# One new table of fixed instruction orders for the five queues of a top-k attention and two-MLP kernel

## The chip, the cores and the metric

The kernel runs on one core of a Trainium2 chip. The metric is the device time of one execution in microseconds (us), and lower is better. A core has a matrix engine (TensorE, PE in the rows), a vector engine (VectorE, DVE), a scalar engine (ScalarE, ACT), a general engine (GpSimd, POOL) and a queue that here only starts transfers (SyncE, SP). Each of the five runs its own list of instructions strictly in the order in which it stands; they wait for each other through semaphores.

## The reference

Two batches of 8 heads, 576 positions, 64 wide. Every attention row keeps its 32 largest scores; the result then goes through two MLPs, whose weights come as f32.

```python
def _attn_ref(q, k, v):                    # (2, 8, 576, 64)
    scores = scale * np.matmul(q, k.transpose(0, 1, 3, 2))
    kth = np.partition(scores, -32, axis=-1)[..., -32:-31]
    scores = np.where(scores >= kth, scores, -1000000000.0)
    scores = scores - np.max(scores, axis=-1, keepdims=True)
    attn = np.exp(scores)
    attn = attn / (np.sum(attn, axis=-1, keepdims=True) + 1e-09)
    return np.matmul(attn, v)
...
x = attn_out.transpose(0, 2, 1, 3).reshape(1152, 512)
h = x @ w_in;  x = np.maximum(0.01 * h, h) @ w_out        # 512 -> 2048 -> 512
h = x @ w_in2; out = (h * np.tanh(softplus(h))) @ w_out2  # 512 -> 2048 -> 512
```

## The kernel before

The 1152 tokens are cut into nine tiles of 128. For each tile the kernel makes the scores of eight heads, so there are 72 (tile, head) steps. Matrix products run on f16 halves: an f32 operand is split into a high and a low f16 part, and three f16 products stand for one f32 product. So each product of the MLPs comes as three lines: L822 to L824 (tile `ph`, 128 columns wide, the first layer of an MLP) and L831 to L833 (tile `y`, 512 columns wide, the second layer).

One step goes through all engines. `front` makes the scores on PE (L676, tile `sps`, two halves of 288 columns), and ACT copies them to `sc` (L678). `topk` runs on DVE: four times MAX8 (L691, eight maxima of each row) with three times MATCH_REPLACE8 between them (L694). ACT then takes the exponentials (L714, L715), and for the tiles from the fourth on casts them to f16 (L746, tiles `warena` or `eh`); POOL makes the low half (L747, L748); SP starts a transposing transfer (L754, tile `pts`); and PE multiplies with v (L760 to L764, tile `av`). When eight heads are done, DVE scales the tile to `x` (L778), which is then transposed to `xt` for the MLPs.

Beside the steps, up to about 230 us, the weights are prepared in groups: SP starts a transfer (`load_w`, L379), and ACT (L382), DVE (L389, L392, L395) and POOL (L331, adds) cut the words into parts; what they make lies in `warena`. A transfer needs a free staging place, which the adds of POOL on an earlier group free. The keys, `prep_k`, are normed and split, and for the later head pairs transposed by transfers on SP (L542 and L544, tile `kst`). The queries are read by L594 (`qr`), and keys and values by L501 and L505 (`rawkr`, `rawkv`).

What decides the order on each engine is neither the code order nor a scheduler: at the end of the kernel, `put_in_order(tc, ORDER)` takes for each of the five engines a string of numbers and ties every instruction to the one that the string names before it. A number is the place of an instruction in the order in which the code built it on that engine, and `a+n` stands for n in a row from a on:

```python
for run in runs.split():
    a, n = (run.split("+") + ["1"])[:2]
    for i in made[int(a):int(a) + int(n)]:
        if last is not None:
            tc.add_manual_dep(i, last.name, kind, reason="order")
        last = i
```

Of the kernel before, what the change touches and what calls it, by code (L numbers as in the profile page):

```python
# [19 lines left out]
        """20+2 19 22 25 28 23 29 27 26 24 35 42 36 43 31 30 32 39 41 46 33 44 47 45 40 37 48 38 49+7 57+2 60 56 34 62  # L20
# [4 lines left out]
        189 183 190+2 188 192+2 195+2 194 197+4""",  # L25
    "Activation":
        """1 6 2 7 4 3 5 9 8 20 17 16 45 11 18 10 12 21 46 13 19 14 27 22 15 28 23 47 24 29 39 25 50 40 49 33 48 41+2
# [30 lines left out]
        889 886+3 890+6""",  # L58
    "Pool":
        """0 2+3 6+2 11 28 30 8 10 5 16 34 31 29 15 9 12 33 19 14 32 35 18 20 13 23 17 21 36+2 24 26 39 38 25 60 27 22  # L60
# [1059 lines left out]
```

## Time and profile before

| what | us |
|---|---|
| median of three runs | 668.48 (668.25 to 670.13) |
| the profiled execution | 669.29 |
| its span, first to last instruction | 667.4 |
| around the span | 1.89 |
| mean granted clock of TensorE | 0.982 |

The profile is that of one execution; all times at which something starts are counted from the beginning of its span. The profiled execution is 0.81 us above the median. Matmuls overlap, so a busy PE is not PE at its peak: how full it is shows in the distance from start to start. In a timeline row, the bracket at the end gives how long the engine was idle before the instruction, and what ended that.

### The profile page before, as it was taken

Reading aid. Unit: us, or ns where it says so; the run is one execution under the profiler, and the core shown is the slowest. Engines: PE = TensorE matmul, PEld = TensorE weight load, DVE = VectorE, ACT = ScalarE, POOL = GpSimd, SP = SyncE. Lnnn points to the kernel's source line nnn. Section 1 sums busy time; section 2 is a strip of 40 time slices with the busy share of each in tenths; the row PEclk is TensorE's granted clock in tenths of the full one; section 3 lists DMA queues with packets and bytes.
Section 4 is the critical chain, followed back from the end, with each engine's and each line's share of the span. In section 5 each row is a group of like instructions: output and inputs, shape, how many; then the busy total and the mean of one; then the engine's idle time right before and its main releaser. Section 6 shows DMA issues by size and latency. Waiting matters only on the chain.

```text
span 667.4 us, 16585 instructions
## 1 busy us (share of the span) xinstructions
PE 600.0 (90%) x6420; PEld 438.1 (66%) x6420; DVE 543.4 (81%) x1172; ACT 541.4 (81%) x1011; POOL 397.4 (60%) x594
## 2 busy tenths in 40 slices
PE   3358887998897999989999999999999999999997
PEld 2234545566766887665676769677677787678673
DVE  2987998999999999989988999799999988430122
ACT  5478798999989899879887987898898897861673
POOL 2869895789865656555544665567466557532330
PEclk9999998999897999989999999999999999999999
DMA  8574355364354101643534242433444423420000
GB/s 275 207 257 137 132 189 192 127 192 141 127 193 140 60 26 20 110 75 72 90 74 90 54 86 56 86 68 56 103 84 72 84 54 52 90 33 18 17 2 32
DMA packets 109359, 66.22 MB, mean 99 GB/s; under 512 B 93792, under 2 KB 99936, under 8 KB 109280
## 3 DMA queue, kind: packets, MB, share of 16 engines
q1 hardware_dynamic: 109280, 65.16, 37.9%
q8 instruction: 50, 0.82, 0.5%
q14 instruction: 29, 0.24, 0.1%
HBM read 41.16 MB, written 2.36 MB: 65 GB/s over the span
## 4 chain that ended last, share of the span: by engine, by line
PE 47%; DVE 20%; ACT 12%; DMA 6%; issue 3%; POOL 3%; SPq 1%; POOLq 0%; DVEq 0%; ACTq 0%
DVE top L691 7%; DVE wk L694 7%; PE y L831 6%; PE y L832 6%; PE y L833 6%; PE ph L824 6%; PE ph L823 6%; PE ph L822 6%; PE sps L676 3%; DMA pts<-warena 2%; PE av L733 2%; ACT warena L433 2%; POOL warena L331 1%; DVE warena L395 1%; ACT warena L438 1%
## 5 line engine op out<-in xcount | busy, mean ns | idle before, releaser
L822 PE MATMUL ph<-xt,warena 128*128 128x128 f16 x1152 | 202.8, 221 | 0.8 <-DMA xt<-xp 0.4
L823 PE MATMUL ph<-xt,warena 128*128 128x128 f16 x1152 | 203.3, 221 | 0.0
L824 PE MATMUL ph<-xt,warena 128*128 128x128 f16 x1152 | 203.2, 221 | 0.0
L691 DVE MAX8 top<-wk 128x8 f32<-128x576 f32 x216 | 161.0, 754 | 2.7
L331 POOL TENSOR_TENSOR warena<-warena 128x256 int32<-128x256 int32 x136 | 108.3, 825 | 21.4 <-ACT sc L678 4.3
L822 PEld LDWEIGHTS <-warena 128*128 128x128 f16 x1152 | 114.1, 99 | 6.8 <-DMA xt<-xp 0.7
L823 PEld LDWEIGHTS <-warena 128*128 128x128 f16 x1152 | 113.9, 99 | 6.9 <-issue 1.8
L824 PEld LDWEIGHTS <-warena 128*128 128x128 f16 x1152 | 113.9, 99 | 2.4 <-issue 0.7
L831 PE MATMUL y<-warena,gg 128*128 128x512 f16 x288 | 109.7, 381 | 0.8 <-DVE gg L863 0.8
L833 PE MATMUL y<-warena,gg 128*128 128x512 f16 x288 | 109.7, 381 | 0.0
L832 PE MATMUL y<-warena,gg 128*128 128x512 f16 x288 | 109.7, 381 | 0.0
L694 DVE MATCH_REPLACE8 wk<-top,wk 128x576 f32<-128x576 f32 x144 | 106.8, 742 | 0.0
L676 PE MATMUL sps<-kst,qst 128*128 128x288 f16 (+1 forms) x320 | 63.1, 300 | 18.6 <-ACT sc L678 14.6
L714 ACT ACTIVATE wk<-sc,nb,iv 128x576 f32<-128x576 f32 x72 | 62.4, 868 | 7.9 <-POOL nb L709 7.9
L678 ACT COPY sc<-sps 128x288 f32<-128x288 f32 x144 | 55.5, 396 | 10.4 <-PE sps L676 9.5
L860 DVE SCALAR_TENSOR_TENSOR mc<-mc,gg 128x512 f32<-128x512 f32 x36 | 28.1, 779 | 43.9 <-ACT mc L859 43.8
L691 DVE MAX8 top<-sc 128x8 f32<-128x576 f32 x72 | 53.9, 749 | 9.9 <-ACT sc L678 8.2
L715 ACT ACTIVATE wk<-wk,nb 128x576 f32<-128x576 f32 x72 | 55.7, 774 | 2.4 <-POOL nb L711 1.0
L846 POOL TENSOR_TENSOR gg<-lk,gg 128x512 f16<-128x512 f32 x36 | 42.9, 1193 | 23.8 <-ACT lk L845 23.4
L694 DVE MATCH_REPLACE8 wk<-top,sc 128x576 f32<-128x576 f32 x72 | 53.5, 743 | 0.0
L831 PEld LDWEIGHTS <-gg 128*128 128x128 f16 x288 | 28.3, 98 | 30.5 <-POOL gg L863 1.4
L833 PEld LDWEIGHTS <-gg 128*128 128x128 f16 x288 | 28.3, 98 | 30.4 <-issue 0.7
(186 smaller groups left out, 1428.2 us busy)
## 6 DMA issues: line engine op xcount, KB each, us to landing
warena<-in_moe_w_in_dram SPq DMA_DIRECT2D x16, 1024.0 KB, 5.6
warena<-in_moe_w_out_dram SPq DMA_DIRECT2D x13, 1024.0 KB, 4.9
warena<-in_moe_w_out_dram SPq DMA_DIRECT2D x6, 512.0 KB, 3.3
out_dram<-o SPq DMA_DIRECT2D x9, 256.0 KB, 2.3
qr<-in_q_dram SPq DMA_DIRECT2D x8, 256.0 KB, 3.2
rawkv<-in_v_dram SPq DMA_DIRECT2D x8, 256.0 KB, 3.2
warena<-held SPq DMA_DIRECT2D x8, 256.0 KB, 2.5
rawkr<-in_k_dram SPq DMA_DIRECT2D x6, 256.0 KB, 3.0
```

The costliest lines, as they stand in the source:

```text
L331: nc.gpsimd.tensor_tensor(out=o[:, a:a + PIECE], in0=o[:, a:a + PIECE], in1=x[:, a:a + PIECE], op=ALU.add)
L676: nc.tensor.matmul(sps[p0:p0 + n, :HS], lhsT=lq[:, c, p0:p0 + n], rhs=rk[:, half * HS:(half + 1) * HS], start=(c == 0), stop=(c == 1))
L691: nc.vector.max(out=top[:, 8 * r:8 * r + 8], in_=src)
L694: nc.vector.match_replace(out=wk, in_to_replace=top[:, 8 * r:8 * r + 8], in_values=src, imm_value=NEG)
L714: nc.scalar.activation(e, sc, AF.Prelu, bias=nb[:, 1:2], scale=iv, alpha=1e30)
L715: nc.scalar.activation(e, e, AF.Exp, bias=nb[:, 2:3], accum_out=self.sums[:, h:h + 1])
L822: nc.tensor.matmul(o, lhsT=wb, rhs=xa, start=(c == 0), stop=False)
L823: nc.tensor.matmul(o, lhsT=wa, rhs=xb, start=False, stop=False)
L824: nc.tensor.matmul(o, lhsT=wa, rhs=xa, start=False, stop=(c == KC - 1))
L831: nc.tensor.matmul(y, lhsT=gb, rhs=whi(j), start=(g == 0 and f == 0), stop=False)
L832: nc.tensor.matmul(y, lhsT=ga, rhs=wlo(j), start=False, stop=False)
L833: nc.tensor.matmul(y, lhsT=ga, rhs=whi(j), start=False, stop=(g == FG - 1 and f == 3))
```

## The change

Only the strings in `ORDER` are replaced. They were worked out from three sets of landing times of the transfers at once, where those of before were worked out from one fixed time for each transfer. No instruction is added or removed: SP has 182 entries, ACT 896, POOL 597, DVE 940 and PE 6210 in both tables. The beginnings of two strings:

```diff
 ORDER = {
     "SP":
-        """20+2 19 22 25 28 23 29 27 26 24 35 42 36 43 31 30 32 39 41 46 33 44 47 45 40 37 48 38 49+7 57+2 60 56 34 62
...
+        """22 25 20+2 23 19 26+4 24 35+2 42+2 30 38 37 31 44 32 45+11 33 57+2 56 40 39 34 60 62 59 61 69 63+2
...
     "DVE":
-        """1+3 7 0 5 8 6 10 4 9 21+2 11 17 47+2 23 18+2 12+2 49 15 24 50 16 31 20 30 33 41 43 35 32 45 14 36 25 40 26
...
+        """1+4 7 9 0 5 8 6 10 21+2 11 23+2 47+3 12+2 50 14+2 17 31 18 33 19 16 20 41 30 35+2 32 34 43 40 45 25 42 26 51
...
```

In the first string, 20 and 21 are the two pieces of the first pair of K heads, 19 is the first tile of q, 22 the first pair of V heads and 25 the second pair of K heads: V and the second K now stand ahead of the first K and q, and the eleven transfers ahead of the first weight transfer (35) are the same ones. In the string of DVE, 17 is the first MAX8 and 21 to 24 and 47 to 50 are the conversions of the first four weight transfers: all eight now stand ahead of that MAX8, where two of them did before.

Three more places, in the middle and late part of the program. The numbers behind the names tell tiles of one name apart.

SP, around the transposes of the keys of two later head pairs (`kst_3537`, `kst_3788`) and the `pts` of two attention steps (`pts_3689`, `pts_3824`). Before:

```order
60 L542 DMA_TRANSPOSE kst_3537<-warena_124 128x4x128
61 L544 DMA_TRANSPOSE kst_3537<-aside_3542 128x64
62 L754 DMA_TRANSPOSE pts_3689<-warena_124 128x9x128
63 L542 DMA_TRANSPOSE kst_3537<-aside_3542 128x4x128
64 L542 DMA_TRANSPOSE kst_3788<-aside_3793 128x4x128
65 L544 DMA_TRANSPOSE kst_3788<-aside_3793 128x64
66 L754 DMA_TRANSPOSE pts_3824<-warena_124 128x9x128
67 L542 DMA_TRANSPOSE kst_3788<-warena_124 128x4x128
68 L505 DMA rawkv_3912<-in_v_dram 64x2x64
```
SP in the changed kernel, the same place:

```order
54 L754 DMA_TRANSPOSE pts_3573<-warena_124 128x9x128
55 L754 DMA_TRANSPOSE pts_3689<-warena_124 128x9x128
56 L501 DMA rawkr_3660<-in_k_dram 128x2x256
57 L544 DMA_TRANSPOSE kst_3537<-aside_3542 128x64
58 L594 DMA qr_3919<-in_q_dram 64x8x64 x2
59 L542 DMA_TRANSPOSE kst_3537<-aside_3542 128x4x128
60 L754 DMA_TRANSPOSE pts_3824<-warena_124 128x9x128
61 L501 DMA rawkv_3656<-in_v_dram 128x2x256
62 L505 DMA rawkv_3656<-in_v_dram 64x2x64
63 L544 DMA_TRANSPOSE kst_3788<-aside_3793 128x64
64 L542 DMA_TRANSPOSE kst_3788<-aside_3793 128x4x128
65 L505 DMA rawkr_3916<-in_k_dram 128x2x64
```
`pts_3689` moved ahead of the two transposes from `aside_3542`, and `pts_3824` ahead of the two from `aside_3793`.

PE, at the scores `sps_6311` (of the step whose first MAX8 stands at 423 us in the trace). Before:

```order
6147 L831 LDWEIGHTS gg_5809
6148 L831 MATMUL y_5926<-warena_124,gg_5809 128x512
6149 L832 LDWEIGHTS gg_5809
6150 L832 MATMUL y_5926<-warena_124,gg_5809 128x512
6151 L833 LDWEIGHTS gg_5809
6152 L833 MATMUL y_5926<-warena_124,gg_5809 128x512
6153 L676 LDWEIGHTS qst_6068
6154 L676 MATMUL sps_6311<-kst_3537,qst_6068 128x288
```
PE in the changed kernel:

```order
6032 L676 LDWEIGHTS qst_6068
6033 L676 MATMUL sps_6311<-kst_3537,qst_6068 128x288
6034 L831 LDWEIGHTS gg_5590
6035 L831 MATMUL y_5926<-warena_124,gg_5590 128x512
6036 L832 LDWEIGHTS gg_5590
6037 L832 MATMUL y_5926<-warena_124,gg_5590 128x512
6038 L833 LDWEIGHTS gg_5590
6039 L833 MATMUL y_5926<-warena_124,gg_5590 128x512
```
Both halves of these scores now stand ahead of the `y_5926` matmuls; before, the second one stood behind nineteen of those.

ACT, at the copies of the scores `sc_8947`, whose first MAX8 stands at 561 us in the trace. Before:

```order
788 L678 COPY sc_8831<-sps_8832 128x288
789 L845 ACTIVATE lk_8482<-ph_8433,fac0_1156 128x512
790 L746 CAST warena_124<-wk_8733 128x576
791 L844 ACTIVATE gg_8593<-ph_8543,fac0_1156 128x512
792 L845 ACTIVATE lk_8592<-ph_8543,fac0_1156 128x512
793 L714 ACTIVATE wk_8842<-sc_8722,nb_8965,iv_8236 128x576
794 L678 COPY sc_8947<-sps_8952 128x288
795 L678 COPY sc_8947<-sps_8948 128x288
796 L715 ACTIVATE wk_8842,sums_8518<-wk_8842,nb_8965 128x576
797 L746 CAST eh_5631<-wk_8842 128x576
```
ACT in the changed kernel:

```order
784 L844 ACTIVATE gg_8483<-ph_8433,fac0_1156 128x512
785 L714 ACTIVATE wk_8733<-sc_8609,nb_8849,iv_8236 128x576
786 L845 ACTIVATE lk_8482<-ph_8433,fac0_1156 128x512
787 L678 COPY sc_8947<-sps_8952 128x288
788 L678 COPY sc_8947<-sps_8948 128x288
789 L715 ACTIVATE wk_8733,sums_8518<-wk_8733,nb_8849 128x576
790 L746 CAST warena_124<-wk_8733 128x576
791 L714 ACTIVATE wk_8842<-sc_8722,nb_8965,iv_8236 128x576
792 L844 ACTIVATE gg_8593<-ph_8543,fac0_1156 128x512
793 L845 ACTIVATE lk_8592<-ph_8543,fac0_1156 128x512
794 L715 ACTIVATE wk_8842,sums_8518<-wk_8842,nb_8965 128x576
795 L746 CAST eh_5631<-wk_8842 128x576
```
The two copies moved ahead of L715, L746 and the next L714.

## Rows read from the trace of the kernel before

**Rows 1.** The page's busy us, share of the span, instructions of each engine.
```profile
PE 600.0 (90%) x6420; PEld 438.1 (66%) x6420; DVE 543.4 (81%) x1172; ACT 541.4 (81%) x1011; POOL 397.4 (60%) x594
```

**Rows 2.** Windows: stretch, length, busy us by engine, TensorE clock, DMA share, GB/s.
```profile
0.00:16.00 16.00, 4.34 (x25) 2.94 (x26) 4.31 (x15) 9.20 (x16) 2.80 (x11) 1.00 0.82 268
16.00:574.00 558.00, 506.76 (x5390) 371.90 (x5389) 518.38 (x1117) 481.69 (x911) 364.47 (x546) 0.98 0.41 107
...
360.00:583.70 223.70, 221.66 (x2796) 165.88 (x2796) 201.60 (x437) 192.01 (x375) 134.16 (x214) 1.00 0.38 74
```

**Rows 3.** Timeline, PE near the end: start, us, engine, line, operation [idle before <-releaser].
```profile
639.78 0.22 PE L824 MATMUL ph<-xt,warena 128*128 128x128 f16 x1
...
640.79 0.22 PE L824 MATMUL ph<-xt,warena 128*128 128x128 f16 x1
640.84 0.38 PE L831 MATMUL y<-warena,gg 128*128 128x512 f16 x1
...
643.00 0.38 PE L832 MATMUL y<-warena,gg 128*128 128x512 f16 x1
```

**Rows 4.** Timeline from the last MAX8 to the last matmul.
```profile
573.26 0.76 DVE L691 MAX8 top<-wk 128x8 f32<-128x576 f32 x1
...
579.85 1.30 SPq L754 DMA_TRANSPOSE pts<-warena  x1
...
583.50 0.19 PE L764 MATMUL av<-rawkv,pts 128*128 128x64 f16 x1
...
583.73 0.69 DVE L778 TENSOR_TENSOR x<-av,rec 128x512 f32<-128x512 f32 x1 [3.19 <-PE av L764]
...
663.27 0.38 PE L833 MATMUL y<-warena,gg 128*128 128x512 f16 x1
```

**Rows 5.** Timeline, DVE: instructions that wait at the places of the change.
```profile
12.76 0.69 DVE L389 TENSOR_SCALAR warena<-warena 128x1024 int32<-128x1024 int32 x1 [2.31 <-DMA warena<-in_moe_w_in_dram]
...
15.82 0.76 DVE L691 MAX8 top<-sc 128x8 f32<-128x576 f32 x1 [1.24 <-ACT sc L678]
...
112.25 0.69 DVE L389 TENSOR_SCALAR warena<-warena 128x1024 int32<-128x1024 int32 x1 [1.03 <-DMA warena<-in_moe_w_out_dram]
...
139.42 0.92 DVE L389 TENSOR_SCALAR warena<-warena 128x1024 int32<-128x1024 int32 x1 [0.27 <-DMA warena<-in_moe_w_in_dram]
...
223.24 0.76 DVE L691 MAX8 top<-sc 128x8 f32<-128x576 f32 x1 [1.06 <-ACT sc L678]
...
423.26 0.76 DVE L691 MAX8 top<-sc 128x8 f32<-128x576 f32 x1 [3.74 <-ACT sc L678]
...
561.23 0.76 DVE L691 MAX8 top<-sc 128x8 f32<-128x576 f32 x1 [1.35 <-ACT sc L678]
```

**Rows 6.** Timeline, PE and ACT: the scores that DVE waits for at 423.
```profile
422.31 0.29 PE L676 MATMUL sps<-kst,qst 128*128 128x288 f16 x1
...
422.76 0.40 ACT L678 COPY sc<-sps 128x288 f32<-128x288 f32 x1 [0.66 <-PE sps L676]
```

**Rows 7.** Timeline, SP and PE: two transposes of exponentials, and who waits.
```profile
279.11 1.29 SPq L754 DMA_TRANSPOSE pts<-warena  x1
...
284.27 0.20 PE L760 MATMUL av<-halves,pts 128*128 128x64 f16 x1 [1.38 <-DMA pts<-warena]
...
289.48 1.31 SPq L754 DMA_TRANSPOSE pts<-warena  x1
...
294.44 0.20 PE L760 MATMUL av<-halves,pts 128*128 128x64 f16 x1 [1.91 <-DMA pts<-warena]
```

**Rows 8.** Timeline, POOL and SP: what the weights used at 139 wait for.
```profile
129.13 1.44 POOL L331 TENSOR_TENSOR warena<-warena 128x256 int32<-128x256 int32 x2 [1.20 <-ACT warena L433]
...
133.69 0.37 SPq L379 DMA_DIRECT2D warena<-in_moe_w_in_dram  x1
```

More of the change, by code (lines that the diff above doesn't have):

```diff
@@ L19 @@
     "SP":
-        """20+2 19 22 25 28 23 29 27 26 24 35 42 36 43 31 30 32 39 41 46 33 44 47 45 40 37 48 38 49+7 57+2 60 56 34 62
[4 rows of a table removed]
-        189 183 190+2 188 192+2 195+2 194 197+4""",
-    "Activation":
-        """1 6 2 7 4 3 5 9 8 20 17 16 45 11 18 10 12 21 46 13 19 14 27 22 15 28 23 47 24 29 39 25 50 40 49 33 48 41+2
[30 rows of a table removed]
-        889 886+3 890+6""",
-    "Pool":
-        """0 2+3 6+2 11 28 30 8 10 5 16 34 31 29 15 9 12 33 19 14 32 35 18 20 13 23 17 21 36+2 24 26 39 38 25 60 27 22
[19 rows of a table removed]
-        579 581 580 584 582+2 585+6""",
-    "DVE":
-        """1+3 7 0 5 8 6 10 4 9 21+2 11 17 47+2 23 18+2 12+2 49 15 24 50 16 31 20 30 33 41 43 35 32 45 14 36 25 40 26
[32 rows of a table removed]
-        935 917+2 921+2 924 919 923 920 925+6 932 931 933+2 936+4""",
-    "PE":
-        """0+19 40+2 38+2 42+2 19+8 44+2 27+6 57+4 33+5 46 71+8 47+5 96+4 79+9 135+16 88 151 90 61+4 89 160+17 91+2
[54 rows of a table removed]
-        5991+3 6042+12 6102+12 6054+48 6114+96""",
+        """22 25 20+2 23 19 26+4 24 35+2 42+2 30 38 37 31 44 32 45+11 33 57+2 56 40 39 34 60 62 59 61 69 63+2 68 67 73
[4 rows of a table added]
+        186 185 187 183 189+2 188 191+3 195+2 194 197+4""",
+    "Activation":
+        """1 6 2 7 4 3 5 9 8 20 16 10+2 45+2 17 12 18+2 21 13+2 27+2 22 15 29 47 23 39 30 24+2 40 33 41 48+2 31 35 34
[29 rows of a table added]
+        865 868+4 874+2 879+2 876+3 881+5 889 886+3 890+6""",
+    "Pool":
+        """0 2+3 8 5+2 12 15 31 28 32+2 29 10 9 7 14 11 13 19 17 30 16 18 20 23 35 24 34 21+2 37 26 39 25 36 38 60 40
[19 rows of a table added]
+        574+2 578 576+2 579+3 584 582+2 585 587 586 588+3""",
+    "DVE":
+        """1+4 7 9 0 5 8 6 10 21+2 11 23+2 47+3 12+2 50 14+2 17 31 18 33 19 16 20 41 30 35+2 32 34 43 40 45 25 42 26 51
[32 rows of a table added]
+        900 891 901 903 899 902 916 935 917+2 921+2 924 923 919 913 925 920 926+9 936+4""",
+    "PE":
+        """0+27 40+2 38+2 27 42+4 28+5 57+4 33+5 46 96+2 71+17 47+5 98+2 88 90 61+4 91 89 52+5 135+16 92 151 94 93
[55 rows of a table added]
+        5825+36 5921+12 5982+11 5934+34 5994+12 5968+14 6006+12 5993 6018+36 6102+12 6054+48 6114+96""",
 }
```

278 rows, old and new, of the table ORDER are left out of this document.

## The prediction

> **What bounds the kernel.** I read the busy shares first. PE is busy 90% of the span, DVE 81%, ACT 81%, POOL 60% [rows 1]; the reader should see that no engine is full on average and that the average decides nothing. The windows by stage show more: from 16 to 574 us DVE is busy 518.38 of 558.00, so it idles 39.6 us in all, and from 360 to 583.7 PE is busy 221.66 of 223.70 [rows 2]. Busy PE isn't yet full PE, so I looked at the distance of its matmuls near the end, where nothing else is left to do: 18 products of the first layer in 1.01 us (0.056 each) and 10 of the second in 2.16 us (0.216 each) [rows 3]. Between 360 and the end I find the same distances almost everywhere in the timeline, so from there on PE has no slack that an order could fill.
>
> The end then shows how the two engines meet. The last MAX8 starts at 573.26; ACT, POOL and a transposing transfer issued at 579.85 follow; the last `av` matmul starts at 583.50, DVE makes the last `x` at 583.73, and PE goes on with stored MLP work to 663.27 [rows 4]. The `av` matmuls that wait for that last head stand in PE's list just where PE arrives: if DVE came a microsecond later, PE would stand still; if DVE came earlier, PE would still have its list to work through. So two chains end together: DVE's top-k chain plus the PE work behind the last `av`, and PE's own list plus its stalls. The time falls only if both get shorter, and rises if either gets longer. That is the rule for the sum.
>
> **The change, part by part.** Nothing is added or removed on any engine, so no term is a work term; every term is a wait that goes, comes or is hidden. I followed both tables through the program. The milestones (ends of top-k, of the weight groups, of each token tile) have the same work of their own engine ahead of them within a few us, and the last MAX8 has the same work on DVE ahead of it. So the new schedule is the old one with local moves, and I price those on which an idle row of before stands.
>
> *Start.* V and the second K, two transfers of 256 KB, go ahead of the first K and q. In the first 16 us the transfers move 268 GB/s [rows 2], so 0.52 MB in front delay K and q by up to 2.0 us. That lies beside DVE's wait of 2.31 us for the first weights at 12.76 [rows 5], which depends on the same eleven transfers as before. The first MAX8 waited 1.24 us for scores at 15.82 [rows 5]; with all eight conversions ahead of it this wait goes, and DVE waits instead for the weights that land one after the other. I take 0; the ends are −1.2 (the wait goes and nothing comes) and +2.3 (a new wait as long as the one for the first weights). The Trainium skill, page "DMA: Bandwidth & Descriptors", section "Two DMAs through the same engine are not ordered", says that descriptors of one queue start in order but are pipelined. By that rule the K and q behind V would overlap with it rather than queue for the full 2.0 us; nothing in the sum depends on it.
>
> *DVE, four waits that go.* At 112.25 DVE waited 1.03 us for a weight transfer [rows 5]; the POOL add that frees its place stands 3.3 us of work earlier now and DVE's conversion 2.2 us earlier, so the wait goes: −1.0. At 223.24 it waited 1.06 for a score copy [rows 5]; the MAX8 stands 2.3 us later in DVE's list, behind other work: −1.1. At 423.26 it waited 3.74 [rows 5]. The copy on ACT had waited 0.66 for the second half of the scores, which PE reached at 422.31 [rows 6], behind nineteen second-layer matmuls (19 × 0.216 = 4.1 us). PE now has both halves before them, and ACT's copy stands 2.0 us of work earlier. PE's side would give all 3.7 back, ACT's only 2.0 less what it waits for other things: I take −1.8, ends 0 and −3.7. At 561.23 it waited 1.35 [rows 5], the copies stand ahead of L715, L746 and L714 on ACT: −1.4. Together −5.3.
>
> *DVE, a wait that comes.* The weights converted at 139.42 waited 0.27 us [rows 5]. Their transfer was issued at 133.69; the adds that free its place began at 129.13 [rows 8] and ended 1.44 later, at 130.57. They now stand 3.9 us of POOL work later, so they end near 134.5, 0.8 us after the old issue, and DVE comes to the conversion 1.1 us earlier: 0.27 + 0.8 + 1.1 = 2.2. What is queued behind the conversion on DVE are the top-k steps of that stretch, and the copies, exponentials and transfers wait for those. Ends 0 (if POOL gets there early, as it idles 40% of the span) and +2.2. I take +2.2, since the transfer took its full time before and nothing covers it.
>
> *SP.* The two `pts` transfers that were issued at 279.11 and 289.48 stood behind transposes of keys, and PE waited 1.38 and 1.91 us for them [rows 7]. They now stand ahead of those: up to −3.3 on PE's chain, and 0 on DVE's, which doesn't wait for PE there. Lost cover: the key transposes come later, and the scores that need them stand far behind in the program, so I price this at 0; if one were late, the MAX8 behind it would wait some 2.6 us, two issues of the 1.3 us that such a transfer takes on SP [rows 7].
>
> *The tail.* Behind the last `av` PE now has 672 first-layer and 194 second-layer matmuls where it had 660 and 192: 12 × 0.056 + 2 × 0.216 = +1.1 on the DVE chain, 0 on PE's, which has the same total.
>
> *Sum.* DVE chain: 0 − 5.3 + 2.2 + 1.1 = −2.0. PE chain: −3.3, which is more than DVE's, so DVE's decides: 669.29 − 2.0 = 667.3 for an execution like the profiled one. That one was 0.81 above the median of 668.48, so in terms of the median 666.5. Ends of this case: with all of the gains and no new wait PE's chain decides, −3.3 or a little beyond with other small stalls, 664; with 423.26 giving nothing, −0.2, 668.3.
>
> A rule that speaks otherwise on what bounds the kernel: the Trainium skill, page "Perfetto Trace Analysis", section "Identifying the Most-Contended Engine", judges TensorE by how busy its weight loads are, not by its matmuls. Those are 66% here against DVE's 81% [rows 1], so by the rule DVE alone would be the bound and PE's stalls would be free; by the distances [rows 3] PE is full after 360. As DVE's chain decides in my sum too, both give −2.0; they part only in the first rival.
>
> **The rivals.** *PE keeps the time (no change).* PE's list is full after 360, so DVE's gains at 423 and 561 (−3.2 of the −5.3) only make DVE wait longer at the end, and if the two `pts` gains at 284 and 294 aren't realised (the transfers share the same queue, and new stalls of the same size appear as every list is reshuffled), PE ends where it did: 668.5. For it: 221.66 of 223.70 [rows 2]. Against: the two waits of PE are plain in the rows.
>
> *Weights late (slower).* Place: the conversions between 139 and 161. The adds on POOL stand later in the new list for several groups there, so transfers are issued later. The one at 139 costs 2.2; the next two by the same reckoning 1.2 and 1.4 where DVE arrives ahead of its data. With the tail's 1.1 that is +5.9; if of the gains only the two before that or close to it arrive (−2.1), +3.8: 672.3. It decides from the point at which the transfers land later than DVE has other work in front of the conversion, and PE, which has no products of the second MLP before its weights are there, can't catch up after 360. For it: DVE has only 0.27 us of slack at 139. Against: a landing that is known to vary would be planned for with more distance, and DVE's other lists there show none.
>
> *More than the sum.* My priced places hold 9.3 of DVE's 39.6 us of idle time. If small waits elsewhere shrink by a tenth more (3 us) and PE's stalls before 360 with them, the time comes to 662 or 663, and with a fifth to 659. Nothing in the rows singles out where; it is what is left when many rows move a little.
>
> **How the numbers follow.** Three tenths of a per cent, 2.0 us, is about what a measurement of this kernel can tell from no change: faster is below 666.5, slower above 670.5. My sum lies on the edge of it. Chances: the sum 0.46 (664 to 668.3, of which 0.30 below the edge), more than the sum 0.13 (658 to 664), PE keeps the time 0.14, weights late or another late transfer 0.27 (670.5 to 677). So faster 0.43, same 0.30, slower 0.27. The range takes in the sum, no change, most of the larger gain and the slower case with its price and one more wait of some 2 us: 660 to 674.5.
>
> **What would show it.** Right: DVE's waits near 112, 223, 423 and 561 gone or below half of what they were; PE's waits on `pts` near 284 and 294 gone; a wait of about 2 us for weights near 138; the last MAX8 about 3 us earlier, and about 1 us more from the last `av` to the end. If the last MAX8 comes 3 us earlier and PE's last `av` doesn't, PE is the bound and the first rival holds. If the waits for weights between 139 and 161 sum to more than 5 us, the second does. The prediction is wrong above all if a new wait of several us stands at a place where before had none, since I could only price places where a row shows something.

## The result: 653.1 us instead of 669.3

| | before | changed |
|---|---|---|
| median, us | 669.31 (668.25 to 671.83, 4 runs) | 653.11 (650.59 to 654.86, 4 runs) |
| ratio, 95% interval | | 0.975 (0.9706 to 0.9794) |
| span of the profiled execution, us | 667.4 | 651.3 |
| mean granted clock | 0.982 | 0.987 |

The kernel is 16 us faster. I forecast 2 us, and the range ended at 660.

The busy shares of the changed kernel hardly differ from those of before [rows 1]:

```profile
PE 594.3 (91%) x6420; PEld 434.6 (67%) x6420; DVE 541.7 (83%) x1172; ACT 540.2 (83%) x1011; POOL 400.7 (62%) x594
```

The windows [rows 2] show a little more. DVE is busy 520.59 us between 16 and 574 us, 2.2 more than before, though its last MAX8 now lies 18 us ahead of 574; PE is full after 360 us as it was:

```profile
0.00:16.00 16.00, 3.28 (x23) 2.60 (x24) 4.92 (x15) 7.64 (x13) 3.06 (x11) 1.00 0.81 270
16.00:574.00 558.00, 518.38 (x5610) 380.63 (x5608) 520.59 (x1127) 494.86 (x936) 376.72 (x560) 0.98 0.43 108
...
360.00:583.70 223.70, 221.84 (x2772) 165.66 (x2771) 196.40 (x421) 190.77 (x372) 132.30 (x208) 1.00 0.37 69
```

The timeline of the end [rows 4] shows everything shifted by nearly one amount: the last MAX8 by 17.8 us, the last `av` by 17.3, the last matmul by 16.1.

```profile
555.44 0.76 DVE L691 MAX8 top<-wk 128x8 f32<-128x576 f32 x1
...
561.24 1.29 SPq L754 DMA_TRANSPOSE pts<-warena  x1
...
566.23 0.19 PE L764 MATMUL av<-rawkv,pts 128*128 128x64 f16 x1
...
566.46 0.69 DVE L778 TENSOR_TENSOR x<-av,rec 128x512 f32<-128x512 f32 x1 [0.31 <-PE av L764]
...
647.18 0.38 PE L833 MATMUL y<-warena,gg 128*128 128x512 f16 x1
```

DVE met PE again here within a fraction of a microsecond (0.31 us of waiting before `x`). What I called the tail grew from 79.77 (663.27 − 583.50) to 80.95 us (647.18 − 566.23), so by 1.2, as forecast.

Next, the instructions on DVE at which waits were priced [rows 5]. The same instructions, at the times at which they start now:

```profile
12.91 0.69 DVE L389 TENSOR_SCALAR warena<-warena 128x1024 int32<-128x1024 int32 x1 [1.03 <-DMA warena<-in_moe_w_in_dram]
...
23.82 0.75 DVE L691 MAX8 top<-sc 128x8 f32<-128x576 f32 x1
...
104.83 0.68 DVE L389 TENSOR_SCALAR warena<-warena 128x1024 int32<-128x1024 int32 x1
...
133.81 0.69 DVE L389 TENSOR_SCALAR warena<-warena 128x1024 int32<-128x1024 int32 x1
...
218.99 0.74 DVE L691 MAX8 top<-sc 128x8 f32<-128x576 f32 x1
...
403.65 0.75 DVE L691 MAX8 top<-sc 128x8 f32<-128x576 f32 x1
...
542.52 0.75 DVE L691 MAX8 top<-sc 128x8 f32<-128x576 f32 x1
```

All waits but the one for the first weights (2.31 before, 1.03 now) are gone, also the one at 139.42 that I took to grow to 2.2 us. And so are most of those behind the first 16 us that I hadn't priced. Three of them in before, and then the same three instructions now:

```profile
285.47 1.35 DVE L540 SCALAR_TENSOR_TENSOR aside<-rawkr,ks,aside 128x320 f16<-128x320 f32 x1 [1.44 <-ACT aside L539]
...
301.31 0.48 DVE L615 SCALAR_TENSOR_TENSOR qn<-qr,qs,qn 128x256 f16<-128x256 f32 x1 [1.62 <-ACT qn L614]
...
353.87 0.16 DVE L264 TENSOR_SCALAR u<-tot 128x1 int32<-128x1 int32 x1 [2.07 <-PE tot L285]
```

```profile
278.25 0.55 DVE L540 SCALAR_TENSOR_TENSOR aside<-rawkr,ks,aside 128x320 f16<-128x320 f32 x1 [0.30 <-ACT aside L539]
...
288.54 0.47 DVE L615 SCALAR_TENSOR_TENSOR qn<-qr,qs,qn 128x256 f16<-128x256 f32 x1
...
343.14 0.14 DVE L264 TENSOR_SCALAR u<-tot 128x1 int32<-128x1 int32 x1
```

I added up the idle time ahead of each of DVE's instructions up to the end of the last MAX8. Waits of over 0.4 us were 28 with 37.6 us in all; now they are 19 with 20.1, so 17.5 less. The shorter gaps grew by 1.5, and DVE's busy time up to there shrank by 1.8; together that is the 17.8 by which the last MAX8 came earlier. This is bookkeeping and doesn't yet say which of the waits cost time: 5.7 of the 17.5 us lie behind 365 us of before, where PE is full.

PE, which is full at the end, has the same 6420 matmuls in both traces. Its idle time fell from 67.4 (667.4 − 600.0) to 57.0 us (651.3 − 594.3) and its busy time from 600.0 to 594.3: 10.4 and 5.7 us make the 16.1.

The SP transfers of [rows 7 and 8] and the matmuls that waited for two of them:

```profile
126.56 0.37 SPq L379 DMA_DIRECT2D warena<-in_moe_w_in_dram  x1
...
269.22 1.30 SPq L754 DMA_TRANSPOSE pts<-warena  x1
...
273.62 0.19 PE L760 MATMUL av<-halves,pts 128*128 128x64 f16 x1
...
275.58 1.27 SPq L754 DMA_TRANSPOSE pts<-warena  x1
...
280.32 0.19 PE L760 MATMUL av<-halves,pts 128*128 128x64 f16 x1
```

The weights' transfer is issued 7.1 us earlier than in before (133.69), and the two `pts` transfers 9.9 and 13.9 earlier; their `av` matmuls follow without a wait. Between 220 and 360 us PE had five waits of over 0.4 us, 6.7 us together; now it has none there.

Where does the lead come from? I took the start of each instruction in both traces, and for the instructions of DVE that lay in each 20 us of before the median difference. I call it DVE's lead when the instructions come earlier. It is −3 us from 40 to 60, about −4 from 100 to 200 (−2.5 to −4.8), −8 by 240 to 280, −12.8 at 300 to 320, −14.7 at 360 to 380, and then −15 to −18 to the end. PE shows about the same steps. So nearly all of the gain was made before about 370 us, where neither engine was full. At 360 to 380 us, 10.5 us of the lead are less idle time ahead of the instructions and about 4 are less busy time: nearly the same instructions stand ahead of them, but those were shorter. The operation at 285.47 above, for one, took 1.35 us in before and takes 0.55 now. What made them shorter isn't shown.

### The profile page after: what moved, and what is told of

It reads as the page before. It is cut to its first block, busy times and chain, and to the rows that moved or that the text cites. A ratio compares the mean times of both kernels' runs of the same rounds, so it can differ in the third digit from the quotient of the medians.

```text
span 651.3 us, 16588 instructions
## 1 busy us (share of the span) xinstructions
PE 594.3 (91%) x6420; PEld 434.6 (67%) x6420; DVE 541.7 (83%) x1172; ACT 540.2 (83%) x1011; POOL 400.7 (62%) x594
## 4 chain that ended last, share of the span: by engine, by line
PE 51%; DVE 21%; ACT 18%; issue 4%; DMA 3%; POOL 1%; SPq 1%; POOLq 0%; DVEq 0%; ACTq 0%
DVE top L691 7%; PE ph L822 7%; PE ph L824 7%; PE ph L823 7%; DVE wk L694 7%; PE y L831 6%; PE y L833 6%; PE y L832 6%; PE sps L676 3%; ACT wk L715 2%; DVE warena L395 2%; PE lp L436 2%; DMA rawkr<-in_k_dram 1%; ACT sc L678 1%; DVE warena L389 1%
## 5 line engine op out<-in xcount | busy, mean ns | idle before, releaser
L676 PE MATMUL sps<-kst,qst 128*128 128x288 f16 (+1 forms) x320 | 64.3, 299 | 11.7 <-ACT sc L678 10.3
L714 ACT ACTIVATE wk<-sc,nb,iv 128x576 f32<-128x576 f32 x72 | 62.5, 868 | 13.4 <-POOL nb L709 13.3
L860 DVE SCALAR_TENSOR_TENSOR mc<-mc,gg 128x512 f32<-128x512 f32 x36 | 26.5, 736 | 45.0 <-ACT mc L859 44.8
L715 ACT ACTIVATE wk<-wk,nb 128x576 f32<-128x576 f32 x72 | 56.1, 779 | 4.3 <-POOL nb L711 2.9
L709 POOL TENSOR_SCALAR nb<-top,iv 128x2 f32<-128x2 f32 x72 | 25.6, 356 | 39.0 <-DVE top L691 31.3
L831 PEld LDWEIGHTS <-gg 128*128 128x128 f16 x288 | 28.3, 98 | 31.0 <-issue 2.1
```

Of the source, the lines that this page charges most:

```text
L676: nc.tensor.matmul(sps[p0:p0 + n, :HS], lhsT=lq[:, c, p0:p0 + n], rhs=rk[:, half * HS:(half + 1) * HS], start=(c == 0), stop=(c == 1))
L714: nc.scalar.activation(e, sc, AF.Prelu, bias=nb[:, 1:2], scale=iv, alpha=1e30)
L715: nc.scalar.activation(e, e, AF.Exp, bias=nb[:, 2:3], accum_out=self.sums[:, h:h + 1])
L831: nc.tensor.matmul(y, lhsT=gb, rhs=whi(j), start=(g == 0 and f == 0), stop=False)
```

## The experiments

**How mixed tables are made.** Most kernels here join the two tables at a seam. "New to 300" means: on every engine, first the instructions that the changed kernel starts before 300 us of its trace, in the new order, then all the rest in the old order. Both parts keep the order in which they ran on the chip, so no list waits in a circle. All five engines have their seam at the same place. The edit touches only the strings (which order 895 of ACT's and 590 of POOL's instructions; the counts of 896 and 597 entries given with the change were too high). In the edits below the tables are named and not printed. A kernel's line numbers shift by up to two, since its strings are longer or shorter (L675 or L677 is then L676 of before). The ratio is to the kernel before on the same chip.

| kernel | new order from/to (us) | median, us | ratio (95%) | lowest to highest |
|---|---|---|---|---|
| new to 110 | 0 to 110 | 671.39 | 1.0029 (0.9999 to 1.006) | 666.9 to 676.3 |
| new to 150 | 0 to 150 | 666.99 | 0.9965 (0.9938 to 0.9991) | 663.3 to 672.2 |
| new to 200 | 0 to 200 | 664.67 | 0.9919 (0.9893 to 0.9945) | 663.3 to 665.7 |
| new to 300 | 0 to 300 | 661.38 | 0.9873 (0.9843 to 0.9903) | 658.9 to 661.6 |
| new to 365 | 0 to 365 | 655.54 | 0.9776 (0.9747 to 0.9806) | 653.6 to 655.8 |
| old to 24 | 24 to end | 653.49 | 0.9761 (0.9734 to 0.9789) | 653.1 to 654.8 |
| old to 60 | 60 to end | 654.77 | 0.9792 (0.9763 to 0.9821) | 651.7 to 657.5 |
| old to 85 | 85 to end | 656.58 | 0.9817 (0.9789 to 0.9846) | 655.4 to 658.6 |
| old to 114 | 114 to end | 660.16 | 0.9859 (0.9822 to 0.9897) | 655.4 to 663.0 |
| old to 312 | 312 to end | 667.22 | 0.9964 (0.9942 to 0.9986) | 664.8 to 669.5 |
| middle | 205 to 365 | 662.40 | 0.9881 (0.9853 to 0.9909) | 660.2 to 663.8 |
| middle, SP old | 205 to 365, four engines | 672.48 | 1.0036 (1.0015 to 1.0057) | 670.5 to 675.5 |
| 205 to 300 | 205 to 300 | 666.00 | 0.9938 (0.9908 to 0.9968) | 661.6 to 671.5 |
| 114 to 200 | 114 to 200 | 671.19 | 1.0003 (0.9972 to 1.0034) | 666.1 to 677.7 |

My theory after the first look: the waits of DVE and PE before about 365 us made the gain, and the late moves, which I had priced at 3.2 us, are worth nothing since PE is full. The rival: the late moves count.

### Late moves: new to 300, old to 312, new to 365

```diff
-    each engine: old table
+    each engine: new table for what starts before 300 us, old table for the rest
```

> The new order for everything that starts before 300 us in the trace of the changed kernel, the old order for all the rest. Theory (the gain is made before about 300 us, where waits of DVE and PE go; after that PE is full, so later moves are worth nothing): nearly the whole gain stays, 653 to 656 us, and the MAX8 that waited 3.7 us at 423 waits again without costing time. Rival (the late moves that I priced at 423 and 561 count, 3.2 to 5.1 us): 656.5 to 659.

```diff
-    each engine: old table
+    each engine: old table for what starts before 312 us, new table for the rest
```

> The counterpart: the old order for everything that starts before 312 us in the trace of the kernel before, the new order for the rest. Theory: 666 to 670 us, as the kernel before, though the wait of 3.7 us at 423 goes. Rival: 664 to 666.

New to 300 gave 661.4 and old to 312 gave 667.2: 8.5 and 2.4 us less by the ratios. The second lies in the theory's range. Its 2.4 us arise around the point at which PE becomes full: DVE was 1.3 us behind before at 340 to 360 us and 1.7 ahead at 380 to 400. At 420 to 440, where the wait of 3.74 us is gone, its lead is 3.6 us, and at 440 to 460 it is 1.9 again. The first fits neither theory nor rival: it should have kept nearly everything. DVE's lead over before was 12.5 us at 300 to 320 us and 7.5 from 360 on. What it lost there shows in its timeline: twice PE waits for a transpose of keys.

```profile
320.07 0.28 PE L675 MATMUL sps<-kst,qst 128*64 128x288 f16 x1 [1.93 <-DMA kst<-warena]
...
343.28 0.31 PE L675 MATMUL sps<-kst,qst 128*64 128x288 f16 x1 [1.79 <-DMA kst<-warena]
```

And in the stretch from 300 to 380 us the clock column is 0.96, where before had 1.00:

```profile
300.00:380.00 80.00, 75.88 (x926) 54.75 (x924) 67.15 (x156) 63.12 (x127) 40.80 (x68) 0.96 0.39 79
```

So the old order of the stretch from 300 to 365 takes back 5.0 of the 12.5 us, or the seam itself does; this run can't tell the two apart. That called for a seam behind the stretch:

```diff
-    each engine: old table
+    each engine: new table for what starts before 365 us, old table for the rest
```

> The new order for everything that the changed kernel starts before 365 us, the old order for the rest, in which DVE waits 3.7 us for the scores near 410. Theory (late moves are worth nothing, since PE is full): 652 to 655, as the changed kernel, with that wait back. Rival (the two late waits that I priced at 3.2 us together count): 656 to 659.

655.5, 0.9776; the interval overlaps that of the whole change (0.9706 to 0.9794). The time alone doesn't decide, since 655.5 lies between the two ranges. The trace says more. The two late waits are back in this kernel, with their old length:

```profile
409.17 0.76 DVE L690 MAX8 top<-sc 128x8 f32<-128x576 f32 x1 [3.91 <-ACT sc L677]
...
547.02 0.76 DVE L690 MAX8 top<-sc 128x8 f32<-128x576 f32 x1 [1.36 <-ACT sc L677]
```

Yet DVE's instructions led those of before by 14.3 us at 400 us, by 14.1 at 440, and by 14.0 at the end. In the changed kernel, where that wait is gone, the lead rose from 15.1 (400 to 420 us) to 17.5 (420 to 440) and was back at 15.8 by 460. So a wait of 3.91 us on DVE cost nothing that shows, and its going gave nothing that lasts: PE was full there. The two profiled spans are 2.0 us apart (653.3 and 651.3), and 1.5 us of that, 14.0 against 15.5 of lead, stood at 380 to 400 already, ahead of both waits. The traces speak for the theory; by the times alone the late moves could still be worth 2 us.

### The start: new to 110, old to 114

```diff
-    each engine: old table
+    each engine: new table for what starts before 110 us, old table for the rest
```

> The new order only up to 110 us of the changed kernel's trace, then the old. DVE's same instructions start about 4 us earlier there in the changed kernel. Theory of gains that add up: about 665 (663 to 667). Rival (the lead is a detour that the rest of the old order gives back, since its later waits hang on transfers and on PE): 668 to 670.

```diff
-    each engine: old table
+    each engine: old table for what starts before 114 us, new table for the rest
```

> The old order up to 114 us of the trace of before, then the new. If gains add up: 653 plus 4, about 657 (655 to 659). Rival (the first 110 us do not matter, the rest makes all of it): 652 to 655. Rival (the new order needs the whole start): above 661.

671.4 and 660.2. The first is no gain, which is the rival's case; the second fits none of its three ranges. The lead of the first 110 us is worth about 7 us when the new order follows (660.2 against 653.1) and nothing when the old one does: in the trace of new to 110 it falls from 3.0 us to 0.3 within 20 us of the seam. The parts don't add up across this seam.

### The middle, and SP's part in it

```diff
-    each engine: old table
+    each engine: old table to 205 us, new table to 365 us, old table for the rest
```

> The old order up to 205 us (trace of before), the new order for what the changed kernel starts before 365 us, and the old order again for the rest. Theory (the stretch from 205 to 365 makes about ten of the sixteen us, whatever stands before and behind it): 658 to 661. Rival (the stretch pays only together with the lead from the start): 664 to 669.

```diff
-    SP as in the middle kernel
+    SP: old table; the other four as in the middle kernel
```

> As mid_new, but SP keeps its old order in the middle too: only the other four engines are new between 205 and 365 us. If the middle gain hangs on when SP issues the transposes of keys and exponentials (PE waits on those in before and in the first mixed kernel): 666 to 670. If it is made by the lists of the other engines: 658 to 661.

The middle by itself gave 662.4 (0.9881, 8.0 us), a little short of the range but on the theory's side. With SP's old order it gave 672.5 (1.0015 to 1.0057): no gain at all but a small loss, beyond the range for that case. The view of one line's waits shows who waited for the transposes of exponentials (engine, line, us in all, times). In before:

```profile
  ACT warena L746: 9.5, 9
  PEld L760: 6.3, 5
  PE av L760: 3.8, 3
```

In the middle kernel (its L745 is L746 of before):

```profile
  PEld L759: 1.6, 2
  PE av L759: 1.3, 1
  ACT warena L745: 1.3, 2
```

With SP's old list:

```profile
  ACT warena L745: 7.4, 5
  PEld L759: 6.4, 4
  PE av L759: 5.7, 3
```

Summed over the three rows (PE's loads and matmuls counted apart) that is 19.6, 4.2 and 19.5 us. In the changed kernel that view has no row at all. The chain behind it, as I read the lists, was one that I hadn't followed: ACT stands in its list before L746 until an earlier transpose has read the buffer that it will write, the preparations of K and q (L290, L539, L614) stand behind that on ACT, and DVE stands before the operations that need those. The opposite, SP's new list with old lists on the other four, wasn't tried.

### Repairs on one or two queues

If single waits are what costs, moving their instructions should give the gain back. First my own SP term:

```diff
     "SP":
-        ... 91 99 98 90 93 100 92 103+3 101 ...
+        ... 91 99 98 90 100 93 92 105 103+2 101 ...
```

> The old table with two moves on SP alone: the transposes of exponentials that were issued at 279.11 and 289.48 stand ahead of the key transposes beside them, as in the new order. My term: PE's waits of 1.38 and 1.91 us go, 664 to 666. Rival (the moved key transposes are needed as soon, or DVE's chain decides there): 668 to 671.

```diff
     "DVE":
-        ... 454 434 464+3 433 ... 428 481 447 482 522 488 490 ... 566 546+2 568 570 548+3 ...
+        ... 454 464+2 434 466 433 ... 428 481+2 522 488 447 490 ... 566 568 570 546+5 ...
```

> The old table with three moves on DVE alone: the operations that waited 1.44 us at 285.47, 1.62 at 301.31 and 1.48 at 349.23 for preparations of K and q stand one or two top-k operations later, so that DVE works through the wait. Theory (what is paid in the middle is DVE standing in front of such an operation, one for one): 4.5 us less, 664 to 667. Rival (the preparation itself is late, through transposes that ACT and PE wait for, and the wait only turns up elsewhere): 668 to 671.

```diff
     "SP": as in the first of these
     "DVE": as in the second
```

> The three moves on DVE together with the two moves on SP of an earlier run, everything else old. Theory (each alone leaves the other chain's waits, both together shorten both chains): 4 to 6 us less, 663 to 666. Rival (the middle gain needs the whole lists): 668 to 671.

669.9 (0.9984, 0.9962 to 1.0006), 669.2 (0.9992, 0.9966 to 1.0017) and 668.7 (0.9979, 0.9957 to 1.0002): none differs from before beyond its interval, and all three lie in the ranges of the rivals. In the traces the waits that the moves were aimed at are gone, but those behind them grow: the wait of 2.07 us at 353.87, which no move touched, is 2.67 with the three moves on DVE and 2.89 with all five. The third shows where the wait goes. The `pts` now go first, so the key transposes that read `aside` are issued at 290.70 and 291.96; ACT stands 2.94 us before L290 until they have read it, DVE 3.49 us behind that, and PE 2.75 (2.70 with the two moves on SP alone):

```profile
290.70 1.22 SPq L542 DMA_TRANSPOSE kst<-aside  x1
291.96 2.16 SPq L544 DMA_TRANSPOSE kst<-aside  x1
...
295.35 0.63 ACT L290 ACTIVATE qn<-qr 128x512 bf16<-128x512 f32 x1 [2.94 <-DMA kst<-aside]
...
296.10 0.15 DVE L264 TENSOR_SCALAR u<-qpart 128x1 int32<-128x1 int32 x1 [3.49 <-ACT qn L290]
...
299.09 0.23 PE L633 MATMUL qt<-identh,qn 128*128 128x128 f16 x1 [2.75 <-DVE k_i L271]
```

The key transposes, which I had priced at 0, carry the wait. In the changed kernel the same instructions of ACT and DVE wait for nothing.

### How far each stretch carries

```diff
+    old to 205, new to 300, old
```

> New order only for what lies between 205 us (trace of before) and 300 us (trace of the changed kernel), old before and behind. In the run with the new order up to 365 us the same stretch gained about 7 us. If the old order behind it takes 4 to 5 of them back, as it did where the new order went from the start to 300: 666 to 668. If they stay: 662 to 664.

```diff
+    new to 200, old
```

> The new order up to 200 us of the changed kernel's trace, then the old. In the changed kernel DVE is 4.6 us ahead there. Theory (a lead at a seam is kept): 664 to 667. Rival (the lead of the start is worth nothing until the new middle follows, as in the run cut at 110): 668 to 672.

```diff
+    old to 24, new
```

> The old order for what starts before 24 us in the trace of before (transfers of K, q and V, first weights, first two MAX8), the new order for all the rest. My term for the start was 0 (-1.2 to +2.3): if right, 652 to 655, as the changed kernel. Rival (the first 200 us gain by the order of the first transfers and of the conversions before the first MAX8): 657 to 660.

```diff
+    old to 114, new to 200, old
```

> The new order only for what lies between 114 us (trace of before) and 200 us (trace of the changed kernel), old before and behind. If the gain of 5.5 us of the run with the new order up to 200 us lies in this stretch: 664 to 666. If it lies in the first 110 us and only needs a seam at which the lists fit: 669 to 672.

```diff
+    new to 150, old
```

> The new order up to 150 us of the changed kernel's trace, then the old. If the lead of 4 us of the first 110 us is kept once the seam lies later: 664 to 667. If the stretch from 150 to 200 makes it: 668 to 672.

```diff
+    old to 60, new
```

> The old order for what starts before 60 us in the trace of before, the new order for all the rest. With the seam at 24 us the time is that of the changed kernel, with the seam at 114 us it is 7 us more. If the waits for the weights at 37, 45 and 54 us are what the new order saves (4.2 us of waiting in the trace of before): 657 to 660, and the runs lie further apart, since those landings vary. If the stretch from 60 to 114 us makes it: 652 to 655.

```diff
+    old to 85, new
```

> The same with the seam at 85 us. If nearly all lies before 60 us: the same as with the seam at 60 us, within 2 us. If the loss grows step by step: between that and the 660 us of the seam at 114.

New to 200 is 5.4 us faster than before (664.7), so a lead from the start can be kept, but at this seam; with the seam at 150, 2.3 us are left. The stretch from 114 to 200 alone gives nothing (1.0003). Old to 24 is as fast as the whole change (653.5): the reordered first transfers and the conversions ahead of the first MAX8 are worth nothing that shows. Then the loss grows with the seam: 654.8 at 60, 656.6 at 85, 660.2 at 114. Each single step lies within the intervals, the whole from 24 to 114 doesn't. Old to 60 falls into the range for the case that the three waits for weights at 37, 45 and 54 us (4.2 us in before) are not what is saved: it has the old order there and loses 2 to 3 us by the ratios. So what the first 200 us gain seems spread from about 24 to 114 us, without one place.

The stretch from 205 to 300 gave 4.2 us; its lead of 7.0 at 300 shrank to 5.8 in the old stretch behind it, and to 4.9 at the end. That is 2.1 us lost where I had allowed for 4 to 5.

A last guess at a single cause in the early part: loads of V that SP issues early though they are used late.

```diff
     "SP":
-        ... 31 30 32 39 41 46 33 44 47 45 40 37 48 ... 60 56 34 62 ... 78 71 ...
+        ... 31 30 32 46 33 44 47 45 37 48 ... 60 56 40 39 34 62 ... 78 41 71 ...
```

> The old table with one move on SP alone: three loads of V (256 KB and two of 32 KB) that SP issues between 12.6 and 38 us, and that are needed only much later, stand among the last weight transfers, as in the new order. Theory (they take the transfers' time from the weights that DVE and ACT wait for up to 60 us): 665 to 668, and shorter waits for weights at 37 and 54 us. Rival (the weights wait for their staging places, not for the transfers): 669 to 672.

672.3, 1.0033 (1.0013 to 1.0053): slower, if anything. That theory failed.

### The spread

The last column of the large table holds something else. Kernels whose stretch from 24 to 200 us is in the new order lie within 1.7 to 2.7 us over 6 runs (old to 24, new to 200, 300 and 365), the changed kernel within 4.3 over 4. Kernels with the old order up to 110 us and beyond spread over 3.6 to 13, over 6 to 12 runs, the repairs on one queue included. But 12 runs spread further than 6 by their number alone, and the changed kernel itself, with 4.3, spreads further than the narrowest of these, with 3.6. The traces differ early. In before, DVE waits for this conversion of weights:

```profile
53.87 1.20 DVE L389 TENSOR_SCALAR warena<-warena 128x1024 int32<-128x1024 int32 x1 [2.58 <-POOL warena L331]
```

In the kernel with the three moves on DVE, whose lists up to 280 us are those of before, the same instruction came 4.3 us later, behind a wait of 4.48:

```profile
58.19 0.69 DVE L389 TENSOR_SCALAR warena<-warena 128x1024 int32<-128x1024 int32 x1 [4.48 <-issue]
```

DVE was then 5.5 us behind before at 120 us, with nothing changed until there. (That execution, of 672.77 us, is one of the slowest of its twelve.) So the old order passes on what varies between two executions in the first 60 us. That the new one passes on less, and that it does so because it was worked out from three sets of landing times, isn't shown.

### The clock as a rival

The mean granted clock rose from 0.982 to 0.987 with the change. Before is at the lower of TensorE's two levels for a while after the wait at 294 us; the third figure from the right in this window is the mean:

```profile
290.00:300.00 10.00, 8.10 (x97) 6.22 (x95) 9.29 (x22) 5.93 (x14) 6.12 (x15) 0.83 0.65 108
```

A mean of 0.982 over 667.4 us leaves 12.0 us of clock ungranted and 0.987 over 651.3 leaves 8.5, so the clock can account for at most 3.5 of the 16 us. It is likely less. The kernel with two moves on SP has the same mean clock as the changed one, and no gain beyond its interval. The first line is that of this kernel, the second that of the changed one:

```profile
core 0: 667.8 us, clock 0.987
```

```profile
core 0: 651.3 us, clock 0.987
```

And of the 114 runs of before beside these experiments, 28 had a mean clock of 0.986 or more; their median was 668.67 and the fastest 664.89. So the clock by itself doesn't make the difference.

## Why the prediction was wrong

- *What bounds the kernel:* right in that PE is full after 360 us and DVE's waits behind that are its slack. The run with a seam at 365 has a wait of 3.91 us there that costs nothing that shows. But I broke this rule in the sum: the terms at 423 and 561 (−1.8 and −1.4) lie in that part, and I let DVE's chain decide. Both waits went, and they gave nothing that shows. The rule that I weighed (the Trainium skill, page "Perfetto Trace Analysis", section "Identifying the Most-Contended Engine") names two measures for TensorE, the share of its weight loads and the matmuls' FLOPs over the peak, and I took the first alone. By it TensorE has 165.88 of 223.70 us between 360 and 583.7, which is 74%, against DVE's 201.60, 90% [rows 2], so DVE would be the bound there and the 3.91 us should have cost their length; the run speaks against it. By the second, an estimate from the matmuls' shapes in that stretch and the page's peak of 78.6 TFLOP/s is 93%, and this agrees with the distances of the matmuls.
- *The start, 0:* right. 653.5 us with the old start. Whether K and q overlapped with V or queued behind it, no run here tells.
- *The four waits of DVE:* all of them went, at 112, 223, 423 and 561. Only the first two lie where PE isn't full.
- *The wait that comes at 139, +2.2:* wrong. The transfer was issued at 126.56, 7.1 us earlier, and the conversion waits for nothing. I had read the wrong add: the transfer at 133.69 waited not for the one that ended at 130.57 but for the last of the four pieces, which POOL began 1.3 us later; it ended at 133.67, right ahead of the issue:

```profile
131.91 1.76 POOL L331 TENSOR_TENSOR warena<-warena 128x256 int32<-128x256 int32 x1
```

And I had turned a place in POOL's list ("3.9 us of POOL work later") into a time, though POOL idled 40% of the span; the add that began at 129.13 came 4.0 us earlier (125.10), and the last of the four ended at 126.53.
- *SP, −3.3 on PE's chain:* the waits went, but the price was wrong in both directions. Alone, the two moves give 0.9984. With the three moves on DVE beside them, the key transposes, which I took at 0, bring a wait of 2.9 us on ACT and 3.5 on DVE. Together with the other lists, SP's order decides 10 us in the middle: 662.4 with it and 672.5 without it.
- *The tail, +1.1:* right, 1.2.
- *The step that failed:* "the new schedule is the old one with local moves, and I price those on which an idle row of before stands". All other waits stood in the sum at 0: those at 37, 45, 54, 104, 241, 285, 301, 349, 354 and 548 us among them, since no single move there explained them. All ten went too (the same instructions wait 0.31 us at most). In the terms of the sum, DVE's chain up to the last MAX8 came to −17.8 us where I had −3.1: −7.2 by the four priced waits (I had −5.3), −0.3 at 139 (I had +2.2), −0.6 in the first 16 us, −7.9 by idle time at places that I hadn't priced, less the new waits, and −1.8 by shorter instructions (both at 0). PE's chain, priced at −3.3, came to −16.1. The seams show what of this counts: the order of all five lists before 365 us keeps nearly all of the gain (655.5 us), while none of the three repairs of waits on one or two queues gives a gain beyond its interval. There a wait that was removed turned up at the next list.
- *The rival "more than the sum"* named this and stopped too early: it took a fifth of the idle time outside the priced places, 6 us, and the net fall there was 7.9, a quarter. Its figures don't follow from its own steps: the priced places hold 7.5 us by [rows 5] between 16 and 574 us (1.03, 0.27, 1.06, 3.74 and 1.35) and not 9.3, and from 666.5 a tenth and a fifth give 663.5 and 660.4.
- *The first rival* (PE keeps the time) had it right that the gains at 423 and 561 are worth nothing, and failed at its other condition: PE's stalls before 360 us shrank as well. *The second* (weights late between 139 and 161) has no row in the trace.

What stays open: which single waits between 24 and 114 us carry their part; why the lead of the first 110 us is lost at a seam there and kept at 200; and what made PE's busy time 5.7 us and DVE's instructions some us shorter. The seams place the gain; they don't resolve it further, since a seam can cost something of its own.

## What to carry to other kernels

When a whole table of orders is replaced, don't price the waits one by one and take the rest at nothing: add up the long waits of the critical engines in the part where no engine is full, and let the range reach for a good part of them. Here DVE's waits of over 0.4 us up to 365 us were 30.0 us, and 11.7 of them went; one case gives no rule for the share. Waits that lie where another engine is already full are slack, however long they look. And a wait at the head of an in-order list belongs to everything that stands behind it; follow it back through the other lists to the queue that starts it before pricing a repair on one of them.

## What I had not expected of the hardware

Two executions, of two kernels with the same instructions in the same order up to 280 us, were 5.5 us apart by 120 us, through one wait of 2.58 us in one and 4.48 in the other and smaller differences around it. And the same instruction of DVE can take 1.20 us in one execution and 0.69 in another, as the conversion of weights above; DVE's 1172 instructions were busy for 543.4 us in before and for 536.2 in new to 300. What sets either apart isn't shown here.
